# The first block in halves of 256 columns, with its loads and transposes interleaved, and the last tile in two pieces instead of three

## Chip, cores and metric

The kernel runs on one core of one Trainium2 chip. The metric is the device time of one execution in microseconds (us), lower is better. Before the change the median of the first three runs was 291.56 us (291.02 to 291.71). The profiler's span, from the first to the last instruction, is about 1.8 us shorter than the device time of the same run. There is one core, so no slow die.

## The reference

```python
# x (1, 2048, 576), w1 (576, 4608), b1 (4608,), w2 (4608, 576), b2 (576,), all bf16
h = einsum("bsd,df->bsf", x, w1) + b1
h = where(h > 0, h, 0) ** 2
out = einsum("bsf,fd->bsd", h, w2) + b2
```

## The kernel before

The 2048 rows are worked in four blocks of 512. A block's x is needed transposed (`xT`, feature on the partitions). The later blocks get it by DMA transpose (5.3 us from issue to landing, by the page); for block 0 TensorE makes it: warm-up matmuls first, then 20 transposes of 128x128 into PSUM, copies to `xT`, and the first matmuls with the weights `w1n` (576 features = four full chunks of 128, k = 0 to 3, and a rest of 64 in `w1n8`). Then comes the long "row stage" (`w_h`, pairs of 64-row matmuls). In the profile `ta` and `tb` are the transposes, `pn` the first matmuls, `ph` the row stage, `po` the second layer.

```python
WARM = [512] * 6 + [256]
for i, n in enumerate(WARM):
    keep(nc.tensor.matmul(wps[:, 0:n], lhsT=ones[:, 0:P], rhs=ones[:, 0:n], start=True, stop=True))
# ...
load_x(nc.sync, 0)
load_x(nc.scalar, 1)
load_x(nc.sync, 2)
load_x(nc.scalar, 3)
for k in range(NK):            # NK = 4
    load_w1n(nc.sync, k)
# ... b1, w1n8 and b2 on the GpSimd queue
for j in range(RT):            # RT = 4 tiles of 128 rows
    cols = slice(j * P, (j + 1) * P)
    ta = ps_h.tile([P, 3, P], BF16, name="ta", tag="ph")
    for i in range(3):
        keep(nc.tensor.transpose(ta[:, i, :], xs[:, j, i * P:(i + 1) * P], ident[:]))
    keep(nc.vector.tensor_copy(out=xT0[:, O:O + 3, cols], in_=ta[:, :, :]))
    # ... tb: two more transposes, copied by ScalarE
# ... a_full(0, "k_outer"):
for k in range(NK):
    for g in range(G):         # G = 4 banks
        full(g, k, k == 0, False)      # 128 x 512 columns
    if k == 1:
        make_b1T()
# ... the last tile of the second layer:
EDGES = [0, 224, 384, 512]
```

Of the kernel before, what the change touches and what calls it, by code (L numbers as in the profile page):

```python
# [11 lines left out]
BF16 = mybir.dt.bfloat16  # L12
# [5 lines left out]
def kernel(  # L18
# [9 lines left out]
    nc = tc.nc  # L28
    keep = tc.keep_in_program_order
    P = 128  # L30
# [3 lines left out]
    S, D = x2.shape  # L34
# [3 lines left out]
    NK = NC // 2  # L38
# [5 lines left out]
    SB = 512  # L44
    RT = SB // P
# [10 lines left out]
    ps_h = ctx.enter_context(tc.tile_pool(name="ps_h", bufs=4, space=PSUM))  # L56
    ps_o = ctx.enter_context(tc.tile_pool(name="ps_o", bufs=4, space=PSUM))

    wps = ps_o.tile([P, 512], FP32, name="wps", tag="po")
    ones = nc.const_aps.tensor(1.0, [P, 512], BF16)  # L60
    WARM = [512] * 6 + [256]
    for i, n in enumerate(WARM):
        keep(nc.tensor.matmul(wps[:, 0:n], lhsT=ones[:, 0:P], rhs=ones[:, 0:n], start=True, stop=True))  # L63

    xs = const.tile([P, RT, D], BF16, name="x_sb")
    w1n = wpool.tile([P, NK, GW], BF16, name="w1n")
# [4 lines left out]
    def load_x(eng, rt):  # L71
        keep(eng.dma_start(out=xs[:, rt, :], in_=x2[rt * P:(rt + 1) * P, :]))

    def load_w1n(eng, k):
        keep(eng.dma_start(out=w1n[:, k, :], in_=w1[k * P:(k + 1) * P, 0:GW]))

    def load_w1n8(eng, h):
        src = w1[NK * P:D, 0:GW].rearrange("p (i h f) -> p i h f", h=2, f=P)
        keep(eng.dma_start(out=w1n8[h * H:(h + 1) * H, :, :], in_=src[:, :, h, :]))

    def load_w1(eng, h, j0, j1):
        keep(eng.dma_start(out=w1_h[h * H:(h + 1) * H, :, j0 * P:j1 * P],
                      in_=w1_v[:, :, GW + h * FH + j0 * P:GW + h * FH + j1 * P]))

    load_x(nc.sync, 0)
    load_x(nc.scalar, 1)
    load_x(nc.sync, 2)
    load_x(nc.scalar, 3)
    for k in range(NK):
        load_w1n(nc.sync, k)  # L90

    ident = const.tile([P, P], BF16, name="ident")
# [1 line left out]
    b1_rows = const.tile([P, P], BF16, name="b1_rows")  # L94
    nc.gpsimd.memset(b1_rows[:], 0.0)
    nc.gpsimd.dma_start(out=b1_rows[0:NFT, :], in_=b1.rearrange("(ft p) -> ft p", p=P))
    load_w1n8(nc.gpsimd, 0)
    load_w1n8(nc.gpsimd, 1)
    b2_col = const.tile([P, 1], BF16, name="b2_col")
    for h in range(2):  # L100
        nc.gpsimd.dma_start(out=b2_col[h * DT:(h + 1) * DT, :], in_=b2[DM:D].rearrange("(d o) -> d o", o=1))
# [5 lines left out]
    E3, O, SPC, E = 0, 1, 5, 6  # L107
# [7 lines left out]
    def alloc_xT(sb):  # L115
        xT_blk[sb] = xtpool.tile([P, NC, SB], BF16, name="xTw", tag="xTw")

    def dup_windows(sb):
        xT = xT_blk[sb]
        keep(nc.vector.tensor_copy(out=xT[0:H, SPC:SPC + 4, :], in_=xT[H:P, E3:E3 + 4, :]))  # L120
        keep(nc.vector.tensor_copy(out=xT[H:P, SPC:SPC + 4, :], in_=xT[0:H, O:O + 4, :]))  # L121

    def load_xT(sb):
        alloc_xT(sb)
        xT = xT_blk[sb]
        rows = x2[sb * SB:(sb + 1) * SB, :]
        keep(nc.sync.dma_start_transpose(out=xT[:, O:O + NK, :], in_=rows[:, 0:P * NK]))
        keep(nc.sync.dma_start_transpose(out=xT[:, E3:E3 + 1, :], in_=rows[:, D - P:D]))
# [9 lines left out]

    alloc_xT(0)
    xT0 = xT_blk[0]  # L140
    for j in range(RT):
        cols = slice(j * P, (j + 1) * P)
        ta = ps_h.tile([P, 3, P], BF16, name="ta", tag="ph")
        for i in range(3):
            keep(nc.tensor.transpose(ta[:, i, :], xs[:, j, i * P:(i + 1) * P], ident[:]))  # L145
        keep(nc.vector.tensor_copy(out=xT0[:, O:O + 3, cols], in_=ta[:, :, :]))  # L146
        tb = ps_o.tile([P, 2, P], BF16, name="tb", tag="po")
        keep(nc.tensor.transpose(tb[:, 0, :], xs[:, j, 3 * P:4 * P], ident[:]))  # L148
        keep(nc.tensor.transpose(tb[:, 1, :], xs[:, j, D - P:D], ident[:]))  # L149
        keep(nc.scalar.copy(out=xT0[:, O + 3, cols], in_=tb[:, 0, :]))  # L150
        keep(nc.scalar.copy(out=xT0[:, E3, cols], in_=tb[:, 1, :]))  # L151
    dup_windows(0)

    b1T = const.tile([P, NFT], FP32, name="b1T")

    def make_b1T():
        b1T_ps = ps_o.tile([P, P], BF16, name="b1T_ps", tag="po")
        keep(nc.tensor.transpose(b1T_ps[:], b1_rows[:], ident[:]))  # L158
        keep(nc.vector.tensor_copy(out=b1T[:], in_=b1T_ps[:, 0:NFT]))
# [6 lines left out]
    def evac_h(sb, bank, ft):  # L166
        r = rpool.tile([P, SB], BF16, name="r", tag="r")
        keep(nc.scalar.activation(out=r[:], in_=bank[:], func=ACT.Relu, bias=b1T[:, ft:ft + 1], scale=1.0))  # L168
        keep(nc.vector.tensor_tensor(out=hTs[sb][:, ft, :], in0=r[:], in1=r[:], op=ALU.mult))  # L169
# [17 lines left out]
    def a_full(sb, order):  # L187
        xT = xT_blk[sb]
        banks = []
        for g in range(G):  # L190
            pool, tag = (ps_o, "po") if g < 2 else (ps_h, "ph")
            banks.append(pool.tile([P, SB], FP32, name="pn", tag=tag))

        def pair(i, start, stop):
            keep(nc.tensor.matmul(banks[2 * i][:], lhsT=w1n8[0:H, i, :], rhs=xT[0:H, SPC, :],  # L195
                             start=start, stop=stop))
            keep(nc.tensor.matmul(banks[2 * i + 1][:], lhsT=w1n8[H:P, i, :], rhs=xT[H:P, E3, :],  # L197
                             start=start, stop=stop))

        def full(g, k, start, stop):  # L200
            keep(nc.tensor.matmul(banks[g][:], lhsT=w1n[:, k, g * P:(g + 1) * P], rhs=xT[:, O + k, :],  # L201
                             start=start, stop=stop))

        if order == "rows_first":
            for i in (1, 0):
                pair(i, True, False)
            for g in (2, 3, 0, 1):
                for k in range(NK):
                    full(g, k, False, k == NK - 1)
                evac_h(sb, banks[g], g)  # L210
        else:
            if order == "k_outer":
                for k in range(NK):
                    for g in range(G):
                        full(g, k, k == 0, False)
                    if k == 1:
                        make_b1T()
            else:
                for g in (2, 3, 0, 1):
                    for k in range(NK):  # L220
                        full(g, k, k == 0, False)
            for i in (1, 0):
                pair(i, False, True)
                evac_h(sb, banks[2 * i], 2 * i)
                evac_h(sb, banks[2 * i + 1], 2 * i + 1)
# [3 lines left out]
        ft_order += [G + j, G + NJ + j]  # L229

    t_order = ft_order[G:] + ft_order[:G]
    EDGES = [0, 224, 384, 512]

    def phase_t(sb):
        pt = ps_o.tile([P, SB], FP32, name="pt", tag="po")
# [13 lines left out]
    def phase_b(sb, hT, last=False, dups=()):  # L249
        for jj in range(RT):  # L250
# [3 lines left out]
            o_sb = opool.tile([P, DM], BF16, name="o_sb", tag="o_sb")  # L254
            edges = EDGES if last and jj == RT - 1 else [0, DM]
            for d0, d1 in zip(edges, edges[1:]):
# [7 lines left out]
    for (j0, j1) in [(0, 1), (1, 2), (2, 4), (4, 6), (6, 8), (8, 10), (10, 12)]:  # L264
        load_w1(nc.sync, 0, j0, j1)
        load_w1(nc.sync, 1, j0, j1)
    load_xT(1)
    for (j0, j1) in [(12, 14), (14, 16)]:
        load_w1(nc.sync, 0, j0, j1)
# [5 lines left out]

    alloc_hT(0)
    a_full(0, "k_outer")
    a_rows(0, 12, 1)
    alloc_hT(1)
    load_xT(3)  # L280
    a_rows(1)
    a_full(1, "rows_first")
    phase_t(0)
    phase_b(0, hTs[0], dups=(2, 3))
    phase_b(1, hTs[1])
    alloc_hT(2)
    a_full(2, "g_outer")
    a_rows(2)
    alloc_hT(3)
# [35 lines left out]
```

## Time and profile before

| what | value | where it is read |
|---|---|---|
| TensorE busy | 285.7 of 289.7 us | page, part 1 |
| chain that ended last | 98% TensorE | page, part 4 |
| first transpose | 3.61 us, when x0 has landed | timeline |
| TensorE idle before the first `pn` | 0.59 us | timeline |
| row stage begins | 10.00 us | timeline |

From the page of the kernel before: the busy line of part 1, the clock row of part 2 (tenths of full speed in 40 slices of 7.2 us), and the head of part 4.

```profile
PE 285.7 (99%) x2052; PEld 134.1 (46%) x2052; DVE 79.7 (28%) x175; ACT 95.7 (33%) x156; POOL 4.2 (1%) x13
PEclk9999999999999999999999999999999999999999
PE 98%; ACT 0%; DVE 0%; issue 0%
```

TensorE is the limit from end to end, so a saving can only come from its two ends. The clock row reads 9 from the first slice on, yet the timeline shows the early matmuls at half speed.

From the timeline of TensorE of the kernel before (columns: start, duration, engine, line, operation, operands, shapes, count, and in brackets the idle time and what ended it):

```profile
3.61 0.50 PE L145 MATMUL ta<-ident,x_sb 128*128 128x128 bf16 x3
4.44 0.31 PE L148 MATMUL tb<-ident,x_sb 128*128 128x128 bf16 x1
5.31 0.22 PE L149 MATMUL tb<-ident,x_sb 128*128 128x128 bf16 x1
5.96 1.46 PE L201 MATMUL pn<-xTw,w1n 128*128 128x512 bf16 x6 [0.43 <-ACT xTw L150]
10.00 0.38 PE L180 MATMUL ph<-xTw,w_h 64*128 64x512 bf16 x1
```

The last line, from a later window, is the first matmul of the row stage. A transpose takes 0.31 us at first and 0.22 us later: between them, at 4.97 us by the trace's clock record, the clock rose from half to full. The last transpose starts at 5.31 us, and TensorE does nothing useful until 5.96 us, because chunk k=0 wants all 512 columns and so the last copy. The bracket counts from the modelled end of a matmul (0.43 us). Below I count a "hole" from start to start, less the streaming time of the matmul before: here 5.957 - 5.308 - 0.056 = 0.59 us.

### The profile page before, as it was taken

Reading aid. Unit: us, or ns where it says so; the run is one execution under the profiler, and the core shown is the slowest. Engines: PE = TensorE matmul, PEld = TensorE weight load, DVE = VectorE, ACT = ScalarE, POOL = GpSimd, SP = SyncE. Lnnn points to the kernel's source line nnn. Section 1 sums busy time; section 2 is a strip of 40 time slices with the busy share of each in tenths; the row PEclk is TensorE's granted clock in tenths of the full one; section 3 lists DMA queues with packets and bytes.
Section 4 is the critical chain, followed back from the end, with each engine's and each line's share of the span. In section 5 each row is a group of like instructions: output and inputs, shape, how many; then the busy total and the mean of one; then the engine's idle time right before and its main releaser. Section 6 shows DMA issues by size and latency. Waiting matters only on the chain.

```text
span 289.7 us, 4742 instructions
## 1 busy us (share of the span) xinstructions
PE 285.7 (99%) x2052; PEld 134.1 (46%) x2052; DVE 79.7 (28%) x175; ACT 95.7 (33%) x156; POOL 4.2 (1%) x13
## 2 busy tenths in 40 slices
PE   8999999999999999999999999999999999999996
PEld 4444444444444444444444444444445444444475
DVE  3444554444502100000025444444440000000001
ACT  4566666666500000000027666666670000000000
POOL 5000000000000000000000000000000000000000
PEclk9999999999999999999999999999999999999999
DMA  7999999400001000000000000000000100000000
GB/s 205 253 227 208 316 391 157 95 0 2 0 20 36 0 18 20 18 18 18 20 18 2 1 2 0 2 0 2 0 2 0 36 20 18 18 18 20 18 20 20
DMA packets 30501, 16.26 MB, mean 56 GB/s; under 512 B 14692, under 2 KB 30448, under 8 KB 30480
## 3 DMA queue, kind: packets, MB, share of 16 engines
q1 hardware_dynamic: 30032, 15.59, 22.4%
q8 instruction: 16, 0.26, 0.4%
q10 hardware_dynamic: 288, 0.30, 0.3%
q0 software_dynamic: 160, 0.08, 0.1%
q14 instruction: 5, 0.04, 0.0%
HBM read 11.36 MB, written 2.36 MB: 47 GB/s over the span
## 4 chain that ended last, share of the span: by engine, by line
PE 98%; ACT 0%; DVE 0%; issue 0%
PE po L259 43%; PE ph L180 42%; PE pt L238 5%; PE pn L201 5%; PE wps L63 1%; PE ph L182 1%; PE pn L195 1%; PE ta L145 0%; ACT xTw L150 0%; ACT xTw L151 0%; DVE o_sb L261 0%; PE tb L149 0%; PE tb L148 0%; PE b1T_ps L158 0%; PE pn L197 0%
## 5 line engine op out<-in xcount | busy, mean ns | idle before, releaser
L259 PE MATMUL po<-w_sb,hT 128*128 128x512 bf16 (+3 forms) x648 | 124.8, 355 | 0.0
L182 PE MATMUL ph<-xTw,w_h 64*128 64x512 bf16 x576 | 124.6, 376 | 0.0
L180 PE MATMUL ph<-xTw,w_h 64*128 64x512 bf16 x576 | 124.6, 376 | 0.0
L168 ACT ACTIVATE r<-ph,b1T 128x512 bf16<-128x512 f32 x128 | 81.1, 685 | 41.6 <-PE ph L182 41.6
L259 PEld LDWEIGHTS <-hT 128*128 128x128 bf16 x648 | 60.7, 98 | 64.3 <-issue 0.8
L180 PEld LDWEIGHTS <-w_h 64*128 64x128 bf16 x576 | 54.1, 94 | 68.3
L169 DVE TENSOR_TENSOR hT<-r 128x512 bf16<-128x512 bf16 x144 | 61.3, 426 | 77.3 <-ACT r L168 76.9
L182 PEld LDWEIGHTS <-w_h 64*128 64x128 bf16 x576 | 54.1, 94 | 0.0
L261 DVE TENSOR_TENSOR o_sb<-po,b_bc 128x512 bf16<-128x512 f32 (+3 forms) x18 | 11.4, 633 | 125.0 <-PE po L259 125.0
L168 ACT ACTIVATE r<-pn,b1T 128x512 bf16<-128x512 f32 x16 | 10.3, 688 | 70.5 <-PE pn L197 69.2
L238 PE MATMUL pt<-hT,w_sb 128*64 128x512 bf16 x144 | 15.9, 380 | 0.0
L201 PE MATMUL pn<-xTw,w1n 128*128 128x512 bf16 x64 | 14.5, 379 | 0.4 <-ACT xTw L150 0.4
L238 PEld LDWEIGHTS <-w_sb 128*64 128x64 bf16 x144 | 8.0, 110 | 7.8 <-issue 0.8
L201 PEld LDWEIGHTS <-w1n 128*128 128x128 bf16 x64 | 6.0, 98 | 8.2 <-issue 1.4
L241 ACT ACTIVATE oT<-pt,b2T 128x512 bf16<-128x512 f32 x2 | 1.4, 687 | 14.5 <-PE pt L238 14.5
L63 PE MATMUL wps<-const-bfloat16-1.0 128*128 128x512 bf16 (+1 forms) x7 | 2.9, 594 | 0.8 <-PEq L309 0.8
L120 DVE COPY xTw<-xTw 64x2048 bf16<-64x2048 bf16 x4 | 2.8, 690 | 0.4 <-ACT xTw L151 0.3
L121 DVE COPY xTw<-xTw 64x2048 bf16<-64x2048 bf16 x4 | 2.7, 686 | 0.1
L146 DVE COPY xTw<-ta 128x384 bf16<-128x384 bf16 x4 | 1.4, 358 | 4.5 <-PE ta L145 4.3
L195 PE MATMUL pn<-xTw,w1n_92 64*128 64x512 bf16 x8 | 2.4, 379 | 0.0
L197 PE MATMUL pn<-xTw,w1n_92 64*128 64x512 bf16 x8 | 2.4, 379 | 0.0
L63 PEld LDWEIGHTS <-const-bfloat16-1.0 128*128 128x128 bf16 x7 | 0.9, 135 | 2.1 <-issue 2.1
(26 smaller groups left out, 16.1 us busy)
## 6 DMA issues: line engine op xcount, KB each, us to landing
w_sb<-in_w_dram SPq DMA_DIRECT2D x6, 864.0 KB, 10.6
w_h<-in_w_dram SPq DMA_DIRECT2D x14, 288.0 KB, 6.3
out_dram<-o_sb SPq DMA_DIRECT2D x15, 128.0 KB, 1.7
w_h<-in_w_dram SPq DMA_DIRECT2D x4, 144.0 KB, 3.5
w1n<-in_w_dram SPq DMA_DIRECT2D x4, 128.0 KB, 3.7
x_sb<-in_x_dram ACTq DMA_DIRECT2D x2, 144.0 KB, 3.2
x_sb<-in_x_dram SPq DMA_DIRECT2D x2, 144.0 KB, 2.9
out_dram<-ot SPq DMA_DIRECT2D x4, 64.0 KB, 1.9
```

The costliest lines, as they stand in the source:

```text
L63: keep(nc.tensor.matmul(wps[:, 0:n], lhsT=ones[:, 0:P], rhs=ones[:, 0:n], start=True, stop=True))
L120: keep(nc.vector.tensor_copy(out=xT[0:H, SPC:SPC + 4, :], in_=xT[H:P, E3:E3 + 4, :]))
L121: keep(nc.vector.tensor_copy(out=xT[H:P, SPC:SPC + 4, :], in_=xT[0:H, O:O + 4, :]))
L168: keep(nc.scalar.activation(out=r[:], in_=bank[:], func=ACT.Relu, bias=b1T[:, ft:ft + 1], scale=1.0))
L169: keep(nc.vector.tensor_tensor(out=hTs[sb][:, ft, :], in0=r[:], in1=r[:], op=ALU.mult))
L180: keep(nc.tensor.matmul(bx[:], lhsT=w1_h[0:H, LO_C[i], jc], rhs=xT[0:H, LO_W[i], :], start=(i == 0), stop=(i == NC - 1)))
L182: keep(nc.tensor.matmul(by[:], lhsT=w1_h[H:P, UP_C[i], jc], rhs=xT[H:P, UP_W[i], :], start=(i == 0), stop=(i == NC - 1)))
L195: keep(nc.tensor.matmul(banks[2 * i][:], lhsT=w1n8[0:H, i, :], rhs=xT[0:H, SPC, :], start=start, stop=stop))
L201: keep(nc.tensor.matmul(banks[g][:], lhsT=w1n[:, k, g * P:(g + 1) * P], rhs=xT[:, O + k, :], start=start, stop=stop))
L238: keep(nc.tensor.matmul(pt[h * DT:(h + 1) * DT, :], lhsT=w2_sb[:, ft, DM:D], rhs=hTs[sb + h][:, ft, :], start=(i == 0), stop=(i == NFT - 1)))
L259: keep(nc.tensor.matmul(po[:, 0:d1 - d0], lhsT=hT[:, ft, jj * P:(jj + 1) * P], rhs=w2_sb[:, ft, d0:d1], start=(i == 0), stop=(i == NFT - 1)))
L261: keep(nc.vector.tensor_tensor(out=o_sb[:, d0:d1], in0=po[:, 0:d1 - d0], in1=b2_bc[:, d0:d1], op=ALU.add))
```

## The change

The intent is to fill that hole. TensorE transposes only x0 and x1 first, begins the weights' matmuls on their 256 columns, and puts the transposes of x2 and x3 between the chunks. The loads are reordered so that each lands about when this order wants it, `w1n8` moves to the Sync queue behind two `w_h` loads, and the last tile is cut into 384 and 128 columns.

```diff
-    WARM = [512] * 6 + [256]
+    WARM = [512] * 6 + [128]
     load_x(nc.sync, 0)
     load_x(nc.scalar, 1)
-    load_x(nc.sync, 2)
-    load_x(nc.scalar, 3)
-    for k in range(NK):
+    load_w1n(nc.sync, 0)
+    load_x(nc.scalar, 2)
+    load_w1n(nc.sync, 1)
+    load_x(nc.sync, 3)
+    for k in range(2, NK):
         load_w1n(nc.sync, k)
     # (cut: w1n8 from the GpSimd queue to the Sync queue; six half banks for the transposes)
-                for k in range(NK):
+                def part(h, k):
+                    hc = slice(h * HS, (h + 1) * HS)          # HS = 256
                     for g in range(G):
-                        full(g, k, k == 0, False)
-                    if k == 1:
-                        make_b1T()
+                        keep(nc.tensor.matmul(banks[g][:, hc], lhsT=w1n[:, k, g * P:(g + 1) * P],
+                                              rhs=xT[:, O + k, hc], start=(h == 0 and k == 0), stop=False,
+                                              skip_group_check=True))
+                # (cut: transposes of x0, x1)
+                x_copies(0)
+                part(0, 0)
+                # (cut: transposes of x2)
+                part(0, 1)
+                part(0, 2)
+                # (cut: transposes of x3)
+                x_copies(1)
+                dup_windows(0)
+                part(0, 3)
+                part(1, 0)
+                make_b1T()
+                for k in range(1, NK):
+                    part(1, k)
-    EDGES = [0, 224, 384, 512]
+    EDGES = [0, 384, 512]
```

Only the very first matmul of a bank has `start=True`, though the second half writes other columns. The Trainium skill, "PSUM — Partial Sum Buffer", section "The four PSUM rules", says why that is right: the first matmul with the start flag clears the accumulate bits of the whole 2 KiB bank, so the second half's first matmul finds clear bits and overwrites.

More of the change, by code (lines that the diff above doesn't have):

```diff
@@ L96 @@
     nc.gpsimd.dma_start(out=b1_rows[0:NFT, :], in_=b1.rearrange("(ft p) -> ft p", p=P))
-    load_w1n8(nc.gpsimd, 0)
-    load_w1n8(nc.gpsimd, 1)
     b2_col = const.tile([P, 1], BF16, name="b2_col")
@@ L140, with x_transpose, x_copies @@
     xT0 = xT_blk[0]
-    for j in range(RT):
-        cols = slice(j * P, (j + 1) * P)
-        ta = ps_h.tile([P, 3, P], BF16, name="ta", tag="ph")
-        for i in range(3):
-            keep(nc.tensor.transpose(ta[:, i, :], xs[:, j, i * P:(i + 1) * P], ident[:]))
-        keep(nc.vector.tensor_copy(out=xT0[:, O:O + 3, cols], in_=ta[:, :, :]))
-        tb = ps_o.tile([P, 2, P], BF16, name="tb", tag="po")
-        keep(nc.tensor.transpose(tb[:, 0, :], xs[:, j, 3 * P:4 * P], ident[:]))
-        keep(nc.tensor.transpose(tb[:, 1, :], xs[:, j, D - P:D], ident[:]))
-        keep(nc.scalar.copy(out=xT0[:, O + 3, cols], in_=tb[:, 0, :]))
-        keep(nc.scalar.copy(out=xT0[:, E3, cols], in_=tb[:, 1, :]))
-    dup_windows(0)
+    HS = SB // 2
+    tb_po = [ps_o.tile([P, 2, HS], BF16, name="tb", tag="po") for _ in range(2)]
+    tb_ph = [ps_h.tile([P, 2, HS], BF16, name="tb", tag="ph") for _ in range(4)]
+    half_banks = [tb_ph, None]
+    def x_transpose(j, k):
+        h, q = divmod(j, 2)
+        qc = slice(q * P, (q + 1) * P)
+        bank, slot, c0 = (half_banks[h][k], 0, k * P) if k < NK else (half_banks[h][2], 1, D - P)
+        keep(nc.tensor.transpose(bank[:, slot, qc], xs[:, j, c0:c0 + P], ident[:]))
+    def x_copies(h):
+        hc = slice(h * HS, (h + 1) * HS)
+        for k in range(NK):
+            src = half_banks[h][k][:, 0, :]
+            if k % 2 == 0:
+                keep(nc.vector.tensor_copy(out=xT0[:, O + k, hc], in_=src))
+            else:
+                keep(nc.scalar.copy(out=xT0[:, O + k, hc], in_=src))
+        keep(nc.vector.tensor_copy(out=xT0[:, E3, hc], in_=half_banks[h][2][:, 1, :]))
     b1T = const.tile([P, NFT], FP32, name="b1T")
@@ L195, in pair @@
             keep(nc.tensor.matmul(banks[2 * i][:], lhsT=w1n8[0:H, i, :], rhs=xT[0:H, SPC, :],
-                             start=start, stop=stop))
+                             start=start, stop=stop, skip_group_check=order == "k_outer"))
             keep(nc.tensor.matmul(banks[2 * i + 1][:], lhsT=w1n8[H:P, i, :], rhs=xT[H:P, E3, :],
-                             start=start, stop=stop))
+                             start=start, stop=stop, skip_group_check=order == "k_outer"))
         def full(g, k, start, stop):
@@ L212, in a_full @@
             if order == "k_outer":
-                for k in range(NK):
+                tb_new = [ps_h.tile([P, 2, HS], BF16, name="tb", tag="ph") for _ in range(2)]
+                half_banks[1] = tb_new + tb_po
+                def part(h, k):
+                    hc = slice(h * HS, (h + 1) * HS)
                     for g in range(G):
-                        full(g, k, k == 0, False)
-                    if k == 1:
-                        make_b1T()
+                        keep(nc.tensor.matmul(banks[g][:, hc], lhsT=w1n[:, k, g * P:(g + 1) * P],
+                                              rhs=xT[:, O + k, hc], start=(h == 0 and k == 0), stop=False,
+                                              skip_group_check=True))
+                for j in range(2):
+                    for k in range(NK):
+                        x_transpose(j, k)
+                for j in range(2):
+                    x_transpose(j, NK)
+                x_copies(0)
+                part(0, 0)
+                for k in range(NK + 1):
+                    x_transpose(2, k)
+                part(0, 1)
+                part(0, 2)
+                for k in range(NK + 1):
+                    x_transpose(3, k)
+                x_copies(1)
[5 more added lines that the diff above has]
+                    part(1, k)
             else:
@@ L266 @@
         load_w1(nc.sync, 1, j0, j1)
+        if j0 == 0:
+            load_w1n8(nc.sync, 0)
+            load_w1n8(nc.sync, 1)
     load_xT(1)
```

## The prediction

> What bounds the kernel now. TensorE does. On the page, PE is busy 285.7 of a 289.7 us span (99%), the granted clock is full in all 40 slices and the chain of work that ended last is 98% PE. From about 10 us to 287 us the timeline shows matmuls at their issue pace without a hole (a pair of 64-row, 512-column matmuls every 0.216 us), so only the ends can give.
>
> The start, by the timeline. The first transpose starts at 3.608 us, released by the landing of x0 (last piece 3.56 us), not by the warm-up. The 20 transposes go at 107 ns each until the clock rises at 4.97 us, then at 56 ns; the last streams out at 5.36 us. PE then idles until 5.957 us: k=0 wants all 512 columns, and waits for the last DVE copy (ends 5.81) and a ScalarE copy (5.605 + 0.284 us). 16 matmuls of 512 columns take 3.45 us, and the row-tiled stage begins at 10.00 us. That hole, 0.59 us, is all that reordering can win.
>
> Costs of the change there. (a) 32 matmuls of 256 columns for 16 of 512: the Trainium skill, "TensorE: Matmul & The Clock Gate", section "Back-to-back issue gap", gives N/2.4 + 2.5 ns; the trace agrees (215.8 ns at 512, 95.8 at 224, 55.9 at 128), so 109 ns each, +0.04 us. (b) x0 and x1 need 10 transposes, stream end 4.65 us. The 256-column DVE copy (about 0.30 us, estimated from 358 ns at 384 columns and 195 at 36) starts after the fifth, near 4.36, so the first matmul starts near 4.72: hole 0.07 us. (c) The second transpose of x2 reuses the PSUM bank that the last of three DVE copies frees, near 5.4 us, while PE arrives near 5.3: hole 0.1 to 0.2 us. (d) w1n k=2 should land at 6.0 to 6.3 us, needed near 6.2: 0 to 0.1 us. (e) w1n8 moves from POOL behind two w1_h loads on SP; landing near 8.5 us (estimate from those loads' 7.5 and 8.0), needed at 9.2: no wait. w1_h for the third row group lands near 12.8, needed at 13.6. (f) The DVE window copies (0.72 us each, done near 9.1) just fit.
> Sum: the row stage begins near 9.7 instead of 10.0 us: -0.3 us (0 to -0.5). The shorter warm-up is worth nothing: x0's landing decides.
>
> The end. Pieces of 224, 160 and 128 columns take 36 x (95.8 + 69.1 + 55.9) ns; 384 and 128 take 36 x (162.5 + 55.9): -0.09 us. The last piece stays 128 wide, so the tail (DVE 0.29 us, store 1.47 us to landing) stays.
>
> Predicted: 291.56 - 0.3 - 0.09, about 291.15 us, 80% range 290.6 to 291.7; run spread before was 291.02 to 291.71. Chances: faster by over 2% 0.005, within 2% 0.99, slower by over 2% 0.005.
>
> Right if: the hole before w1n shrinks from 0.59 to under 0.1 us, the first row-tiled matmul starts at 9.5 to 9.9 us, a hole of 0.1 to 0.2 us stands between the first and second transpose of x2, and the final piece's 36 + 36 matmuls take 7.87 us.
>
> Wrong if: w1n8 or the delayed w1_h loads land after they are needed (a PE wait on a DMA at 9 to 14 us); the clock rises later than 4.97 us, which costs up to half of the delay; copies take longer than estimated; or a late DMA channel holds w1n up.

## The result

The changed kernel takes 291.55 us (median of 6 runs, 291.00 to 291.58), the kernel before in the same rounds 291.63 us (6 runs, 291.02 to 291.91). The ratio is 0.9994, 95% interval 0.9981 to 1.0007: the same. Ratios are the mean time of one kernel's runs over that of the other's of the same rounds, so not quite the ratio of the medians quoted. The outputs are right.

The page of the changed kernel, the same lines as above:

```profile
PE 285.1 (98%) x2017; PEld 133.7 (46%) x2032; DVE 79.5 (27%) x176; ACT 95.2 (33%) x152; POOL 2.8 (1%) x11
PEclk9999999999999999999999999999999999999999
PE 98%; issue 0%; DVE 0%
```

And its TensorE timeline:

```profile
3.49 1.25 PE L150 MATMUL tb<-ident,x_sb 128*128 128x128 bf16 x10
4.59 1.01 PE L228 MATMUL pn<-xTw,w1n 128*128 128x256 bf16 x4
5.40 0.74 PE L150 MATMUL tb<-ident,x_sb 128*128 128x128 bf16 x5
5.93 1.39 PE L228 MATMUL pn<-xTw,w1n 128*128 128x256 bf16 x8
7.16 0.44 PE L150 MATMUL tb<-ident,x_sb 128*128 128x128 bf16 x5
10.21 0.38 PE L189 MATMUL ph<-xTw,w_h 64*128 64x512 bf16 x1
```

There is no bracket: the hole is gone (0.06 us is left of it). Yet the row stage begins at 10.21 us, later than before, and the span is 289.80 us against 289.74. The durations say why. Five transposes take 0.74 us at 5.40 us and 0.44 us at 7.16 us: in this execution the clock rose only at 6.65 us, not at 4.97. TensorE worked without a pause, but 1.7 us longer at half speed.

The end of the two kernels, from their timelines; first before, then changed. The last lines of VectorE are the additions of the pieces of the last tile.

```profile
279.04 0.69 DVE L261 TENSOR_TENSOR o_sb<-po,b_bc 128x512 bf16<-128x512 f32 x1 [7.08 <-PE po L259]
286.99 0.29 DVE L261 TENSOR_TENSOR o_sb<-po,b_bc 128x128 bf16<-128x128 f32 x1 [1.69 <-PE po L259]
```

```profile
279.25 0.69 DVE L295 TENSOR_TENSOR o_sb<-po,b_bc 128x512 bf16<-128x512 f32 x1 [7.08 <-PE po L293]
287.11 0.29 DVE L295 TENSOR_TENSOR o_sb<-po,b_bc 128x128 bf16<-128x128 f32 x1 [1.45 <-PE po L293]
```

From the addition of the last whole tile to that of the last piece: 7.95 us before, 7.86 us after. That is the predicted 0.09 us.

So the question is not where a big gain went. It is what the front of the kernel is worth, when its time depends on something that differs between executions of the same program.

### The profile page after: what moved, and what is told of

Same layout as the page of the kernel before. It is cut to its first block, busy times and chain, and to the rows that moved or that the text cites. A ratio compares the mean times of both kernels' runs of the same rounds, so it can differ in the third digit from the quotient of the medians.

```text
span 289.8 us, 4679 instructions
## 1 busy us (share of the span) xinstructions
PE 285.1 (98%) x2017; PEld 133.7 (46%) x2032; DVE 79.5 (27%) x176; ACT 95.2 (33%) x152; POOL 2.8 (1%) x11
## 4 chain that ended last, share of the span: by engine, by line
PE 98%; issue 0%; DVE 0%
PE po L293 43%; PE ph L189 42%; PE pt L272 5%; PE pn L210 4%; PE pn L228 1%; PE wps L63 1%; PE tb L150 1%; PE ph L191 1%; PE pn L204 1%; DVE o_sb L295 0%; PE b1T_ps L167 0%; PE pn L206 0%
## 5 line engine op out<-in xcount | busy, mean ns | idle before, releaser
L293 PE MATMUL po<-w_sb,hT 128*128 128x512 bf16 (+2 forms) x600 | 123.8, 366 | 0.8 <-issue 0.3
L293 PEld LDWEIGHTS <-hT 128*128 128x128 bf16 x612 | 58.3, 98 | 66.7 <-issue 0.8
L295 DVE TENSOR_TENSOR o_sb<-po,b_bc 128x512 bf16<-128x512 f32 (+2 forms) x17 | 11.2, 660 | 125.0 <-PE po L293 125.0
L177 ACT ACTIVATE r<-pn,b1T 128x512 bf16<-128x512 f32 x16 | 10.3, 687 | 68.7 <-PE pn L206 67.4
L210 PE MATMUL pn<-xTw,w1n 128*128 128x512 bf16 x45 | 10.4, 379 | 0.4 <-issue 0.3
L210 PEld LDWEIGHTS <-w1n 128*128 128x128 bf16 x48 | 4.5, 98 | 6.0 <-issue 0.8
L228 PE MATMUL pn<-xTw,w1n 128*128 128x256 bf16 x32 | 4.8, 304 | 0.0
L228 PEld LDWEIGHTS <-w1n 128*128 128x128 bf16 x32 | 3.4, 110 | 0.6
L157 DVE COPY xTw<-tb 128x256 bf16<-128x256 bf16 x4 | 1.1, 292 | 6.6 <-PE tb L150 6.6
L159 ACT COPY xTw<-tb 128x256 bf16<-128x256 bf16 x4 | 1.3, 375 | 3.7 <-PE tb L150 3.7
```

The source lines that it names most:

```text
L177: keep(nc.scalar.activation(out=r[:], in_=bank[:], func=ACT.Relu, bias=b1T[:, ft:ft + 1], scale=1.0))
L210: keep(nc.tensor.matmul(banks[g][:], lhsT=w1n[:, k, g * P:(g + 1) * P], rhs=xT[:, O + k, :], start=start, stop=stop))
L228: keep(nc.tensor.matmul(banks[g][:, hc], lhsT=w1n[:, k, g * P:(g + 1) * P], rhs=xT[:, O + k, hc], start=(h == 0 and k == 0), stop=False, s ...
L293: keep(nc.tensor.matmul(po[:, 0:d1 - d0], lhsT=hT[:, ft, jj * P:(jj + 1) * P], rhs=w2_sb[:, ft, d0:d1], start=(i == 0), stop=(i == NFT - 1)))
L295: keep(nc.vector.tensor_tensor(out=o_sb[:, d0:d1], in0=po[:, 0:d1 - d0], in1=b2_bc[:, d0:d1], op=ALU.add))
```

## The experiments

My theory A after the first result: the moment at which the clock rises is chance, and each us of half clock costs up to half a us, as much as the change can win. Rival B: the change itself delays the rise. A second question came up with the answer: what limits the front when the clock rises early?

Every run below also took a trace. "Rise" is the first full-clock record of that trace, in us from the span's start.

### 1. Both kernels again, unchanged

No edit.

> The kernel before, unchanged, for a second trace. In its first trace the clock rose at 4.97 us and the span was 289.74 us; in the changed kernel's trace it rose at 6.65 us and the span was 289.80 us. Theory A (the moment of the clock's rise is chance, and every us of delay costs half a us): the rise lies anywhere between about 4.2 and 7.6 us in this trace, and the span is 289.74 + 0.5 x (rise - 4.97) within 0.15 us. Rival B (the change itself delays the rise): the rise is again near 5 us. Under both, an idle hole of 0.5 to 0.65 us stands before the first w1n matmul.

> The changed kernel, unchanged, for a second trace. Theory A: the rise lies anywhere between about 4.2 and 7.6 us, and the span is 289.80 + 0.5 x (rise - 6.65) within 0.15 us; if the rise is early (under 5.3 us), waits of 0.1 to 0.3 us on w1n k=1 or k=2 appear, because TensorE then arrives before they land. Rival B: the rise is again near 6.6 us. Mean over the rounds: A says 0.2 to 0.6 us under the kernel before, B says equal within 0.2 us.

Measured: the kernel before 291.31 us (5 runs, 291.18 to 291.58), ratio to the kernel before 0.9995 (0.9983 to 1.0007). It is the same program, so this row is a control. The changed kernel 291.21 us (5 runs, 290.98 to 291.61), ratio 0.9993 (0.9980 to 1.0006): no further from 1 than the control, within the intervals.

The second trace of the kernel before, TensorE timeline and the wait of its weight loads (waited for: us in total, times, longest):

```profile
3.59 0.34 PE L145 MATMUL ta<-ident,x_sb 128*128 128x128 bf16 x3
4.74 0.22 PE L149 MATMUL tb<-ident,x_sb 128*128 128x128 bf16 x1
5.91 1.47 PE L201 MATMUL pn<-xTw,w1n 128*128 128x512 bf16 x6 [0.94 <-DMA w1n<-in_w_dram]
9.96 0.38 PE L180 MATMUL ph<-xTw,w_h 64*128 64x512 bf16 x1
PEld L201 <- DMA w1n<-in_w_dram: 1.1, 1, 1.1
```

The clock had risen at 3.61 us, with the first transpose. TensorE finished the transposes 0.57 us earlier than in the first trace and gained almost nothing: the hole grew from 0.59 to 1.11 us, and the row stage began at 9.96 instead of 10.00 us. The wait now ends with w1n k=0. Fifteen of its sixteen pieces had landed by 4.79 us, the last at 5.86 us. The Trainium skill, "DMA: Bandwidth & Descriptors", section "Why a DMA increments its semaphore by 16 and not by 1", says that the engines of one DMA finish independently and that only the full count means that all has landed; here one late piece held TensorE until 5.91 us. It did not cost the whole 1.11 us: the copies that the first matmul waited for in the first trace ended here at 5.37 us, so without the piece TensorE would have started near 5.4 us (an estimate), and the piece cost about 0.5 us.

The second trace of the changed kernel, the same two views:

```profile
3.53 0.73 PE L150 MATMUL tb<-ident,x_sb 128*128 128x128 bf16 x10
4.80 0.61 PE L228 MATMUL pn<-xTw,w1n 128*128 128x256 bf16 x4 [0.54 <-DVE xTw L160]
5.25 0.44 PE L150 MATMUL tb<-ident,x_sb 128*128 128x128 bf16 x5
5.53 1.30 PE L228 MATMUL pn<-xTw,w1n 128*128 128x256 bf16 x8
9.72 0.38 PE L189 MATMUL ph<-xTw,w_h 64*128 64x512 bf16 x1
PEld L228 <- DMA w1n<-in_w_dram: 1.1, 2, 0.7
```

The rise was at 3.40 us. Ten transposes took 0.73 us instead of 1.25, and now the changed kernel has holes: 0.70 us before the first `pn` and 0.26 us before chunk k=2. The bracket names VectorE, but the copy that the matmul needs had ended at 4.31 us and the copy of L160 at 4.79 us is none of its inputs; the weight load in front of it waited for w1n k=0, whose fifteenth piece landed at 4.33 and sixteenth at 4.75 us. One of its packets of 1024 bytes took 0.98 us; the median of that size in the first 6.5 us is 0.05 us. The copy alone would have held TensorE to about 4.37 us, so of the 0.70 us about 0.27 belong to the copy and 0.43 to the late piece. And the late piece decided nothing in the end: w1n k=2 landed at 6.17 us and would have held its matmul at 6.22 us all the same, and the row stage begins 3.50 us after that.

Rival B falls: the same changed kernel rose at 6.65 us in one trace and at 3.40 us in another, the kernel before at 4.97 and 3.61. Theory A's first half stands, that the moment differs between executions of one program; its range does not, as both second traces rose before the 4.2 us that it allowed. (That the change shifts the rise a little on the average, so few traces cannot exclude.) Its sum fails: half a us per us of delay foretold spans of 289.06 and 288.17 us; measured were 289.69 and 289.30. An early rise only uncovers the next limit, the copies and the landing of the weights. At nearly the same early rise, the changed kernel's span is 0.38 us shorter (289.69 to 289.30), but as each trace has a late piece, this is no clean comparison.

### 2. An attempt to take the clock out

```diff
-    WARM = [512] * 6 + [256]            # the changed kernel: + [128]
+    WARM = [512] * 24 + [256]
+    for _ in range(3):
+        keep(nc.gpsimd.memset(xs[:], 0.0))
     load_x(nc.sync, 0)
```

> The kernel before with every load of x, and all loads behind them on the same queue, held back about 6 us by memsets on GpSimd, and 24 warm-up matmuls instead of 6, so that the clock has risen before the first transpose. Theory A: the spread of its runs shrinks from 0.9 us to under 0.3 us. If the spread comes from elsewhere, it stays at 0.7 to 0.9 us. From the first transpose to the first row-tiled matmul about 5.9 us (6.39 in the first trace, of which 1.36 us at half clock), with a hole of 0.6 to 1.0 us in it.

> The changed kernel held back in the same way. Theory A: the spread under 0.3 us. With a risen clock TensorE outruns the loads: from the landings in the changed kernel's trace (w1n k=1 2.2 us, k=2 3.0 us, k=3 3.3 us after x0) I work out waits of about 0.5 us on k=1 and 0.3 us on k=2, and 6.3 to 6.5 us from first transpose to first row-tiled matmul: 0.3 to 0.6 us slower than the held-back kernel before. If instead only the hole counts (the naive reading), it is 0.5 to 0.7 us faster.

Measured: 300.72 us (6 runs, 298.30 to 300.95) and 298.72 us (4 runs, 298.64 to 298.95). The spread of the first became larger, not smaller, so this failed as a way to hold the clock fixed. In its trace TensorE stands idle for 1.1 us before the first transpose and for 0.85 and 0.59 us after it, and five of its six runs report a mean granted clock of 0.989 to 0.994, where the run with the trace reports 1.000 and is the fastest: which points to a second stretch of low clock in those (two of the other kernel's four runs report 0.994). The difference of 2 us between the two kernels is then at least in part one of clocks, and I draw nothing from it. In the traces, both at full clock, the front took 6.68 us before and 6.33 us in the changed kernel, where I had expected the latter to be the slower. Behind its front, though, the changed kernel's trace waits 0.90 us for a `w_h` load (until 21.13 us), and the other's does not: the risk named under step (e) of the prediction, come true with the loads held back. Its span is the longer one, 296.83 us against 296.49.

### 3. One half of the change at a time

The first has the new order of loads in the kernel before, and nothing else; the second has all the rest of the change with the old order of loads.

```diff
 # order_only, in the kernel before      # halves_only: the same lines the other way round, in the changed kernel
-    load_x(nc.sync, 2)
-    load_x(nc.scalar, 3)
-    for k in range(NK):
+    load_w1n(nc.sync, 0)
+    load_x(nc.scalar, 2)
+    load_w1n(nc.sync, 1)
+    load_x(nc.sync, 3)
+    for k in range(2, NK):
```

> The kernel before with the new order of loads alone. Theory: the gain needs both parts. Here the first w1n matmul still wants all four blocks of x, and x3, now the fourth load on its queue, lands 1 to 1.5 us later (6.0 in the changed kernel's trace, 4.5 before); copies add 0.87 us. First row-tiled matmul at 10.3 to 10.9 us, 0.3 to 0.9 us slower than the kernel before. If the order of loads alone carried the gain, it would be faster.

> The changed kernel with the old order of loads. Theory: w1n k=0 lands at 4.8 us (5.9 if one packet is slow, as in the second trace of before) where the halves want it at 4.4 to 4.6, and k=1 at 6.0; with an early clock the row stage begins near 10.0 us, as before the change, and with a late clock (over 6 us) near 10.2 us. Mean of the rounds within 0.2 us of the kernel before. If the halves alone carried the gain, it equals the changed kernel.

Measured: order alone 292.39 us, ratio 1.0031 (1.0018 to 1.0044), slower by about 1 us. Halves alone 291.49 us, ratio 1.0024 (0.9993 to 1.0054), with two of six runs at 293.6 and 293.8 us. From the timelines, order alone first (rise 5.48 us), then halves alone (rise 4.25 us):

```profile
6.23 0.34 PE L147 MATMUL ta<-ident,x_sb 128*128 128x128 bf16 x3 [0.88 <-DMA x_sb<-in_x_dram]
7.11 0.38 PE L203 MATMUL pn<-xTw,w1n 128*128 128x512 bf16 x1 [0.43 <-ACT xTw L152]
```

```profile
5.65 0.61 PE L226 MATMUL pn<-xTw,w1n 128*128 128x256 bf16 x4 [1.06 <-DMA w1n<-in_w_dram]
```

With the order alone TensorE waits for x3 and then still for the copies; the row stage begins at 11.16 us, a little later than expected. With the halves alone it waits 1.2 us for w1n k=0, and the row stage begins at 10.43 us, where I had expected about 10.0. So the new order needs the halves. That the halves need the new order is not shown: in their one trace the last two pieces of w1n k=0 were late (fourteen by 4.76 us, then 5.31 and 5.61), and the four other runs have a mean of 291.30 us, no worse than the changed kernel. The two slow runs have no trace; what made them over 2 us longer is open.

### 4. The weights taken out of the way

In block 0 the `pn` matmuls of chunks 0 to 3 multiply by a constant tile. Their outputs are wrong, which doesn't matter for the times. All loads stay.

```diff
-  lhsT=w1n[:, k, g * P:(g + 1) * P]
+  lhsT=ones[:, 0:P]                     # block 0 only
```

> Wrong result on purpose: block 0 of the kernel before multiplies by a constant instead of w1n, so that its first matmuls wait for no weights; all loads are kept. Theory: with an early clock (under 5 us) the hole is set by the copies alone, 0.6 to 0.7 us instead of 1.1, and the row stage begins near 9.5 us (9.96 with weights); with a late clock near 10.5.

> Wrong result on purpose: the same in the changed kernel. Theory (the landing of w1n limits the changed kernel where the clock rises early, half clock limits it where it rises late): with an early clock both holes (0.70 and 0.26 us) shrink to under 0.3 us in sum and the row stage begins at 8.9 to 9.2 us instead of 9.72; with a late clock (over 6 us) it begins at 10.1 to 10.3 as with weights. Rival (the waits on w1n hide nothing, PE or copies limit anyway): 9.6 to 9.8 with an early clock. Mean of the rounds 0.4 to 0.7 us under that of before_freew.

Measured: 291.56 us (mean 291.42 of 5, ratio 1.0000, 0.9988 to 1.0013) and 291.11 us (mean 291.15 of 6, ratio 0.9991, 0.9979 to 1.0003). The difference of the means is 0.27 us, under the 0.4 to 0.7 expected. The rises came at 5.12 and 6.22 us, so neither trace shows the early case that would have decided between the theories. They show a hole of 0.50 us on the copies before, no hole over 0.06 us at the `pn` matmuls of the changed kernel's chunks 0 to 3, and a row stage at 9.95 us (between the 9.5 and 10.5 expected) and 10.04 us (just under the 10.1 to 10.3 expected for a late clock). The changed kernel's trace does show what the weights would have cost in it: w1n k=2 landed at 6.90 us, 0.36 us after TensorE had begun the matmuls that otherwise wait for it (6.54 us). So even with this late rise the load would have held it. Without the wait for weights the changed kernel's mean is 0.23 us under its mean with them (291.38 of 17 runs, neither of the same rounds nor on the same chip), with a standard error of about 0.15: this points to the weights but does not prove their share.

### 5. Half clock through the whole front

```diff
-    WARM = [512] * 6 + [256]            # the changed kernel: + [128]
+    WARM = [128]
```

With nearly no warm-up TensorE first gets busy when x0 lands, so the clock rises late in both kernels.

> The kernel before with one warm-up matmul of 128 columns instead of seven, so that TensorE is first busy when x0 lands and the whole block-0 stage runs at half clock. Theory (busy TensorE raises the clock some 2.6 to 6 us after it first gets busy, and each us at half clock costs about half a us once TensorE is the limit): the rise lies between 6.1 and 9.6 us, the row stage begins at about 10.5 us + 0.5 x (rise - 6.65), a hole of 0.5 to 0.65 us stands before the first w1n matmul, and the runs are 0.5 to 2 us slower than the kernel before. If the rise does not matter, the time equals the kernel before.

> The changed kernel with one warm-up matmul. Theory: the row stage begins at 10.2 us + 0.5 x (rise - 6.65), no hole over 0.12 us in the block-0 stage and no wait for w1n; mean of the rounds 0.3 to 0.5 us under that of before_cold. If the closed hole is given back at half clock, the means are equal within 0.1 us.

Measured: 292.66 us (6 runs, 292.15 to 293.26) and 292.59 us (6 runs, 291.56 to 292.80); the means are 292.66 and 292.38, so 0.28 us apart (0.3 to 0.5 expected), with a standard error of 0.25. The traces say more, since their rises fall equally late, 9.20 and 9.04 us, both 5.55 us after the first transpose. From the timelines, before and then changed:

```profile
3.65 0.50 PE L145 MATMUL ta<-ident,x_sb 128*128 128x128 bf16 x3 [2.61 <-DMA x_sb<-in_x_dram]
5.65 0.31 PE L149 MATMUL tb<-ident,x_sb 128*128 128x128 bf16 x1
6.30 1.44 PE L201 MATMUL pn<-xTw,w1n 128*128 128x512 bf16 x3 [0.33 <-ACT xTw L150]
11.76 0.38 PE L180 MATMUL ph<-xTw,w_h 64*128 64x512 bf16 x1
```

```profile
3.49 1.25 PE L150 MATMUL tb<-ident,x_sb 128*128 128x128 bf16 x10 [2.45 <-DMA x_sb<-in_x_dram]
4.58 1.01 PE L228 MATMUL pn<-xTw,w1n 128*128 128x256 bf16 x4
11.37 0.38 PE L189 MATMUL ph<-xTw,w_h 64*128 64x512 bf16 x1
```

From the expected formulas, with these rises, the row stage would begin at 11.78 and 11.40 us; it does at 11.76 and 11.37. From the first transpose to the row stage it is 8.11 us before and 7.89 us in the changed kernel: 0.22 us won. The hole was 0.54 us long and is 0.06 now, but at half clock it wastes only half as much work: 0.24 us. The additional matmuls cost nothing at half clock (213.3 ns at 256 columns, 426.7 at 512); the half of them behind the rise cost about 0.02 us, which leaves 0.22.

### 6. The changed kernel a third time, and a version with staggered loads

The version comes from experiment 1: x2 follows w1n k=0 on the same queue instead of competing with it.

```diff
     load_w1n(nc.sync, 0)
-    load_x(nc.scalar, 2)
+    load_x(nc.sync, 2)
     load_w1n(nc.sync, 1)
+    load_w1n(nc.sync, 2)
     load_x(nc.sync, 3)
-    for k in range(2, NK):
-        load_w1n(nc.sync, k)
 # ... behind ScalarE's table load:
+    load_w1n(nc.scalar, 3)
```

> The changed kernel once more, for a mean over more runs and a third trace. Theory from the traces: 0.25 to 0.3 us at the start, 0.09 us in the last tile and 0.05 us behind it, 0.35 to 0.45 us in all under the kernel before on the average; the eleven runs so far say 0.11 us with a standard error of 0.09. Over 0.25 us here would say that the first ones fell on late rises; under 0.15 us that something gives back part of it.

> A version that the experiments point to: in the changed kernel x2 follows w1n k=0 on the same queue instead of competing with it from the ScalarE queue, k=2 goes before x3, and k=3 is issued by ScalarE after its table load. Theory: w1n k=0 lands at 4.0 to 4.2 us unless a packet is slow, the hole before the first w1n matmul falls under 0.15 us with an early clock; the mean 0 to 0.2 us under the changed kernel, which five rounds may not tell from nothing. If x2 or x3 now comes too late, a wait on x of over 0.2 us stands in the block-0 stage.

Measured: the changed kernel 291.36 us (6 runs, ratio 0.9997, 0.9984 to 1.0011; its mean is 0.15 us under that of the kernel before on the same chip, at the lower mark of the expectation), the staggered one 291.44 us (5 runs, ratio 0.9996, 0.9983 to 1.0008). The staggered version is no better. From its TensorE timeline (rise 4.84 us):

```profile
4.51 0.74 PE L228 MATMUL pn<-xTw,w1n 128*128 128x256 bf16 x4
5.40 0.45 PE L150 MATMUL tb<-ident,x_sb 128*128 128x128 bf16 x5
6.02 1.05 PE L228 MATMUL pn<-xTw,w1n 128*128 128x256 bf16 x8 [0.17 <-DMA w1n<-in_w_dram]
PEld L150 <- DMA x_sb<-in_x_dram: 0.7, 2, 0.4
PEld L228 <- DMA w1n<-in_w_dram: 0.3, 1, 0.3
```

The hole before the first `pn` is 0.05 us, as hoped; w1n k=0 landed at 4.22 us. But holes of 0.31 us (x2), 0.33 us (w1n k=1, last piece 0.53 us behind the others) and 0.12 us (x3) took its place. Moving a wait is not removing it while the loads are this dense.

## Why the prediction was right or wrong

The traces in one table. "Front" is from the first transpose to the row stage.

| trace | first transpose | rise | row stage | front | holes over 0.12 us |
|---|---|---|---|---|---|
| before | 3.61 | 4.97 | 10.00 | 6.39 | 0.59 copies |
| before, second | 3.59 | 3.61 | 9.96 | 6.37 | 1.11 copies, then w1n k=0 |
| before, no warm-up | 3.65 | 9.20 | 11.76 | 8.11 | 0.54 copies |
| changed | 3.49 | 6.65 | 10.21 | 6.72 | none |
| changed, second | 3.53 | 3.40 | 9.72 | 6.19 | 0.70 copy, then w1n k=0; 0.26 w1n k=2 |
| changed, third | 3.69 | 5.71 | 9.87 | 6.18 | none |
| changed, free weights | 3.55 | 6.22 | 10.04 | 6.48 | none |
| changed, no warm-up | 3.49 | 9.04 | 11.37 | 7.89 | none |

The four traces of the changed kernel without holes (one with free weights) lie on one line, fitted to them: the front is 5.14 us of work at full clock plus half of the time from the first transpose to the rise. It gives 6.72, 6.15, 6.47 and 7.92 us; measured were 6.72, 6.18, 6.48 and 7.89. In the second trace the clock was up from the start, the line would give 5.14, and the front took 6.19: 0.96 us of it are the two holes.

- **The total.** 291.15 us was predicted, 290.6 to 291.7; the median was 291.55, and all of the changed kernel's 17 runs but one (291.87) lie in the range. That says little, as 28 of the 44 runs of the kernel before lie in it too, and so does its median; the range held no change as well. The direction is likely right, the size was too large: over all runs the kernel before has a mean of 291.49 us (44 runs) and the changed one of 291.38 (17 runs), a gain of 0.11 us with a standard error of 0.07, where 0.39 was predicted. Eleven of the 44 ran on a chip on which the changed kernel never did; in the three sets of rounds that have both, the means differ by 0.17, 0.17 and 0.15 us, together 0.16 us with a standard error of 0.08.
- **The end, -0.09 us: exact.** From the row stage's start to the last VectorE addition, five traces with the old pieces give 276.99 us and seven with the new pieces 276.90 (the held-back kernels of experiment 2 left out). A further 0.06 us came unpredicted: from that addition to the end of the span it is 2.73 to 2.75 us with three pieces and 2.67 to 2.69 with two. The Sync queue checks the semaphores of its stores one after another at the end, about 0.06 us each, and with one store fewer the last store uses the semaphore that is checked last, so no check follows it.
- **The hole shrinks to under 0.1 us: right in two of three traces of the changed kernel** (0.06 us). In the third it is 0.70 us.
- **The row stage at 9.5 to 9.9 us: right in two of three** (9.72, 9.87; 10.21 in the first).
- **Step (c), a hole of 0.1 to 0.2 us at the second transpose of x2: wrong.** It is in none of the changed kernel's traces. VectorE freed the bank at 5.27 us instead of 5.4, and TensorE came to the second transpose at 5.50 us instead of 5.3.
- **Step (d), w1n k=2 late by 0 to 0.1 us: right in two traces, 0.26 us in the other.** Step (e), w1n8 and `w_h` in time: right, no wait at either in the changed kernel's three traces (0.90 us at `w_h` in its held-back form).
- **The step that failed is the size of the front, -0.3 us.** I took the rise at 4.97 us as a property of the program and worked out both kernels from it. It was named as a risk, but the sum used one value. The runs put in its place three cases. With a late rise the changed kernel is bound by TensorE at half clock, and the hole was worth half its length: 0.22 us measured. With an early rise TensorE outruns the copies and the loads: the fronts differ by 0.18 us, in traces that both have a late piece. For a rise in between, 1.36 us after the first transpose, the line alone gives a front of 5.82 us against the 6.39 measured before. That number is an estimate; no trace has both kernels there, and it leaves out w1n k=2. That load landed at 6.42, 6.17 and 6.16 us in the changed kernel's three traces, and the row stage begins 3.55 us after its landing where TensorE waits for it (9.72 after 6.17). So with these landings the row stage cannot begin before 9.7 to 10.0 us at any clock, again an estimate: 0 to 0.3 us under the 10.00 before, and not the hole's 0.59. (In the trace without warm-up k=2 landed at 5.86 us, which would allow 9.4.)
- **Missing from the sum: w1n k=0.** I checked k=2 and w1n8 against their landings and took k=0 for granted. It is the load that the changed order wants first, and its last piece held TensorE for 0.43 us in one trace; there k=2 would have taken up that time anyway.

What stays open: the traces say 0.15 us at the end and about 0.2 us or more at the front, and the means say 0.11 +- 0.07 us for all, or 0.16 +- 0.08 where both kernels ran on the same chip. That is less than the traces' sum, by about two standard errors. The timed runs have no trace, so neither their rises nor their late pieces are known; that they were more often late than in the three traces is possible but not shown.

## What to carry to other kernels

A change worth less than the spread of an unchanged kernel's runs has to be judged by the traces, several of each kernel, and compared at like clock; a control that is the same program shows how small a ratio means anything. In the first 10 us ask three questions of each matmul: at which clock does it run, has its input been copied, and has the last of the sixteen pieces of its load landed. Filling one hole moves the limit to the next of the three, and a hole at half clock is worth only half its length.

## What the Trainium skill lacked or had wrong

- "TensorE: Matmul & The Clock Gate", "What you observe", gives the rise of the clock about 4 us into matmul activity, give or take 0.5 us (though a note further down calls the number of slow matmuls run-variable). In the ten traces with the seven warm-up matmuls, which begin at 0.78 us, the rise came between 3.40 and 6.65 us of the span: a range of 3.25 us. The page's own length of the free-running window (3.4 us) fits this range better than its 0.5 us.
- The same page holds the ramp to be under 1% of a span. It is (of the changed kernel's three traces, the one with the latest rise began the row stage 0.49 us later than the one with the earliest), but that exceeds a change of 0.1%, and the page does not say that an early rise need not shorten the kernel: 1.36 us earlier was worth 0.04 us in the kernel before, as the copies and then a load held TensorE.
- The same page's gap of N/2.4 + 2.5 ns holds here also at widths that it does not list: 95.8 ns at 224 columns, 162.5 ns at 384. The page gives it for isolated matmuls and says that a stream of weight loads and matmuls runs at about 81 ns (128 columns) and 131 ns (512). Here such a stream, the second layer, with one weight load for each matmul, runs at 55.8 and 215.9 ns.
- "DMA: Bandwidth & Descriptors", "Latency and other measured facts", gives 0.2 us for an HBM access and 2 us at high load. No page says how often one packet of a load is slow or what that does to a wait: here 11 packets of 1024 bytes of 6144 (the first 6.5 us of twelve traces) took 0.63 to 0.99 us (median 0.05), and the sixteenth piece of a load landed up to 1.07 us after the fifteenth. The section does call two of the sixteen DMA engines, 7 and 15, usually slower than the rest; these traces do not number the engines, so whether the late pieces are theirs is open.
- No page has the end of a program: each semaphore that the Sync queue checks in turn took about 0.06 us (the nearest is "Advanced Engine Details and Errata", "Network/Comms", with 50 to 100 ns for a sequencer's reading of a semaphore, which fits), and which one the last store uses shifts the end by that much.
